# Window attention and two MLPs on one core: the sign of the weights through a parametric ReLU, and the normalising of the first items on VectorE

## The chip, the core and the metric

One core of a Trainium2 chip runs one program. The metric is the device time of one execution in microseconds (us). Three executions of the kernel before took 966.86, 967.08 and 969.48 us; their median, 967.08 us, is the time that the change is held against.

## The reference, cut to what matters

```python
# attention: q, k, v are (4 batches, 8 heads, 576 rows, 64), window 128
scores = scale * q @ k^T + bias[head]          # masked to 0 <= i - j < 128
attn = exp(scores - max(scores));  attn = attn / (sum(attn) + 1e-09)
x = (attn @ v) as 2304 tokens x 512
# first MLP, 512 -> 2048 -> 512; weights are float64
h = x @ w_in;  g = max(h, 0) + alpha * min(h, 0);  x = g @ w_out
# second MLP, 512 -> 2048 -> 512; weights are float64
h = x @ w_in2;  g = h * sigmoid(1.702 * h);  out = g @ w_out2
```

The weights of both MLPs come as float64, and the chip computes in float32. So every weight has to be turned into float32 on the chip before a matmul can use it.

## The kernel before, in words

**Items.** Attention is cut into 64 items: `u` (the first 256 query rows of a batch, or the other 320) by batch by head. Item `n` below 32 has `u` = 0. The first 16 items (`FP`) run their matmuls on plain float32 operands; from item 16 on the operands are split into a high and a low part. An item goes through these steps: `a_qk` (TensorE, scores `s`, L343 or L352 and L353), `a_bias` (VectorE, adds the bias and takes the extreme of each row, L363), `a_exp` (ScalarE, exponential with row sums, L379), `a_recip` (VectorE, L387 and L388), `a_norm` (multiplies the rows by the reciprocal), `a_trans` (TensorE, transposes into `pt`, L412), `a_pt_hi` (ScalarE copies `pt` out of PSUM, L419), `a_av` (TensorE, the product `x` with the values, L433 or L445) and, after each second head, `a_x3` (ScalarE casts the result into `xh`, L480, VectorE makes the low part `xl`, L107). Two heads fill one of four chunks of `xh`; eight items fill the 256 tokens of one batch.

**Normalising.** An item of `u` = 0 has two pieces, 128x128 and 128x256. With `"mix"`, which the first 18 items have, VectorE multiplies the small piece (L399) and ScalarE the large one (L397). With `"dve"`, all other items, VectorE does both (L399).

**Decoding weights.** A layer's weights come in 32 chunks of 128x512 float64, each loaded as pairs of 32-bit words into one of four buffers `ws` (`w_load`, L131, 512 KB). A chunk then goes through: `w_scale` (ScalarE: L147 scales the high words, read as a float, by 2^-112 into `wd`; L148 scales the low words), `w_sign` (VectorE L152: keeps the top bit of the high words alone), `w_shift` (VectorE L157: shifts `wd` left by 3, which moves the exponent into place and pushes the sign out, and ors the kept sign in), `w_add` (VectorE L162: adds the low words; after this the buffer `ws` is free for the next load), and `w_split` (ScalarE L102 or VectorE L103 makes the high part `wh`, VectorE L107 the low part `wl`).

**Stages.** A prologue of ten loop rounds runs ten items and decodes two chunks a round. Then comes the first MLP in blocks `k` of 256 tokens (the last of 512) by 16 slices `f` of the hidden width: twelve matmuls `h` (L494), the activation (ScalarE L509, VectorE L519, ScalarE L523, VectorE L107), twelve matmuls `o` (L545). One attention item goes along with every two slices. The block `k` = 0 needs items 0 to 7 (all four chunks of `xh`) and decodes the last twelve chunks of the first layer on the way; `k` = 1 needs items 8 to 15. The second layer's 32 chunks are decoded during the last block of the first MLP and during the second MLP (`h` L592, later `p` L659).

**What sets the order.** The program is recorded in the order of the code, and a scheduler with a model of the instructions' times then orders each engine's instructions once, when the program is built. On the chip each engine takes them in that order. From the last block of the first MLP on (`pin`), instructions of the decoding keep the order of the code.

Of the kernel before, what the change touches and what calls it, by code (L numbers as in the profile page):

```python
# [11 lines left out]
F32 = mybir.dt.float32  # L12
# [3 lines left out]
AF = mybir.ActivationFunctionType  # L16
ALU = mybir.AluOpType
# [48 lines left out]
def tile_window_attention__then__two_mlps(  # L66
# [13 lines left out]
    nc = tc.nc  # L80
# [32 lines left out]
    def pin(ins):  # L113
        if pinned:
            tc.keep_in_program_order(ins)
# [9 lines left out]
    wst, wtm, wt, wf = {}, {}, {}, {}  # L125
# [8 lines left out]
    def w_words(i):  # L134
        s = wst[i].bitcast(I32).rearrange("p (n t) -> p n t", t=2)
        return s[:, :, 0], s[:, :, 1]

    def w_scale(i):
        lo, hi = w_words(i)
        layer, f, part = chunks[i]  # L140
        if layer == 1 and part == 1:
            if f % 2 == 0:
                wf[f // 2] = p3["wf"].tile([P, 2, DM], I32, tag="wf", name="wf")
            wtm[i] = wf[f // 2][:, f % 2, :]
        else:
            wtm[i] = wtmp.tile([P, DM], I32, tag="wd", name="wd")
        pin(nc.scalar.mul(wtm[i].bitcast(F32), hi.bitcast(F32), 2.0**-112))  # L147
        pin(nc.scalar.mul(lo, lo.bitcast(U32), 2.0**-29))  # L148

    def w_sign(i):  # L150
        lo, hi = w_words(i)
        pin(nc.vector.tensor_scalar(hi, hi, -0x80000000, None, op0=ALU.bitwise_and))  # L152

    def w_shift(i):
        lo, hi = w_words(i)
        w = wtm[i]
        pin(nc.vector.scalar_tensor_tensor(w, w, 3, hi, op0=ALU.logical_shift_left, op1=ALU.bitwise_or))  # L157

    def w_add(i):

# [59 lines left out]

    def w(step, lim=2 * NF):

        names = ("load", "scale", "sign", "shift", "add", "split")
        i = wdone.get(step, 0)
        if i < min(lim, wdone.get(names[names.index(step) - 1], 0)):
            {"scale": w_scale, "sign": w_sign, "shift": w_shift, "add": w_add, "split": w_split}[step](i)
            wdone[step] = i + 1

    def w_ahead():
        if wdone.get("add", 0) >= 2 * NF and ("x", 0) not in p2:  # L230
            return
        i = wdone.get("load", 0)
        while i < min(wdone.get("add", 0) + NST, len(chunks)):
            w_load(i)
            i += 1
        wdone["load"] = i

    def w_decode(lim):
        w("sign", lim)
        w("shift", lim)  # L240
        w("add", lim)
        w_ahead()
        w("scale", lim)
# [79 lines left out]
    @stage  # L323
    def a_split_v(n, b, u, h, U):
        nv = (2, 4)[u]
        vr = raw_of(n)[:, UCOLS[u] - nv * D : UCOLS[u]].rearrange("p (j d) -> p j d", d=D)
        if n < FP:
            d0 = (h % 2) * D
            nc.gpsimd.tensor_copy(vzs[n % 2][:, :, d0 : d0 + D], vr)
            return  # L330
        vp = ar["v", n % 2]
        nc.scalar.copy(vp[:, :nv, :D], vr)
        sub("pool", vp[:, :nv, D:], vr, vp[:, :nv, :D])
# [49 lines left out]
    @stage  # L383
    def a_recip(n, b, u, h, U):
        s = sts[n % 2]
        m = len(U["chunks"])
        nc.vector.tensor_scalar(s[:, 8 : 8 + m], s[:, 4 : 4 + m], 1e-9, None, op0=ALU.add)  # L387
        nc.vector.reciprocal(s[:, 12 : 12 + m], s[:, 8 : 8 + m])  # L388

    @stage  # L390
    def a_norm(n, b, u, h, U, eng):
        tt, s = tts[n % 2], sts[n % 2]
        for i, (c0, rows, kk, keys) in enumerate(U["chunks"]):
            t = tt[:rows, i * 256 : i * 256 + keys]
            r = s[:rows, 12 + i : 13 + i]
            if eng == "act" or (eng == "mix" and i):
                nc.scalar.mul(t, t, r)  # L397
            else:
                nc.vector.tensor_scalar(t, t, r, None, op0=ALU.mult)  # L399
# [27 lines left out]
    @stage  # L427
    def a_av(n, b, u, h, U):
        if n < FP:
            x = st["x", n] = st["x", n - 1] if h % 2 else ps_a.tile([P, 512], F32, tag="a", name="x")  # L430
            pt, vz = pts[n % 2], vzs[n % 2]
            for j in range(2):
                nc.tensor.matmul(  # L433
                    x[:, j * P : 256], vz[:, j, :], pt[:, j * 256 : 256 + j * P],
                    start=(h % 2 == 0 and j == 0), stop=(h % 2 == 1 and j == 1), skip_group_check=True,
                )
            return
        vp = ar["v", n % 2]
        x = ps_a.tile([P, 512], F32, tag="a", name="x")
        js = (0, 1) if u == 0 else (2, 1, 3, 4)  # L440
        for i, j in enumerate(js):
            col, nq, oc = PTCOL[u][j]
            v = vp[:, j - U["k0"] // P, :]
            for k, p in enumerate((ar["pth"], ar["ptl"])):
                nc.tensor.matmul(  # L445
                    x[:, oc : oc + nq], v, p[:, col : col + nq],
                    start=(i == 0 and k == 0), stop=(i == len(js) - 1 and k == 1),
                    skip_group_check=True,
                )
        st["x", n] = x  # L450
# [283 lines left out]
    for n in range(H + 2):  # L734

        a_av(n - 2)
        a_split_v(n)
        if n + 4 < H + 2:
            a_load(n + 4)
        if n >= H:  # L740
            a_load(n + 2)
        if n + 1 < H + 2:
            a_qk(n + 1)
        a_bias(n)
        w("split")
        w("sign")
        a_exp(n)
        a_recip(n - 1)
        w("shift")
        a_norm(n - 1, "mix")  # L750
        a_trans(n - 1)
        w("add")
        w_ahead()
        w("scale")
        a_x3(n - 2)
        w("split")
        w("sign")
        w("shift")
        a_pt_hi(n - 1, 0)
        a_pt_hi(n - 1, 1)  # L760
        if n + 2 < H + 2:
            a_split(n + 2)
        w("add")
        w_ahead()
        w("scale")
    n = H + 2
# [1 line left out]
    for i in range(2):  # L768
        a_pt_lo(n - 2, i)
    a_recip(n - 1)  # L770
    a_norm(n - 1, "mix")
    a_av(n - 2)
    a_x1(n - 2)
    a_x2(n - 2)
# [5 lines left out]
    steps = [(k, f) for k in range(KM + 1) for f in range(NF)]  # L780
    for s, (k, f) in enumerate(steps):
        n = H + 2 + s // 2
        norm = "mix" if k == 0 else "dve"
        if (k, f) == (KM, 0):
            pinned.append(True)
        dec = k == 0 or k == KM
        lim = min(3 * NF, max(W1, wdone["split"]) + 3) if k else W1

        def wd(*names):
            for x in names if dec else ():  # L790
                w(x, lim)

        m = n - 1
        m1_h(k, f)
        if s % 2 == 0:
            a_trans(m)
            a_qk(n)
            a_pt_hi(m, 0)
            m1_n(k, f)
            wd("sign")  # L800
            m1_g(k, f)
            a_pt_hi(m, 1)
            a_bias(n)
            wd("shift")
            a_pt_lo(m, 0)
            a_pt_lo(m, 1)
            wd("add", "scale")
            w_ahead()
            a_split(n + 1)
            a_exp(n)  # L810
            m1_lo(k, f, "dve")
        else:
            a_av(m)
            if n == FP:
                a_parts()
            a_recip(n)
            a_split_v(n)
            a_load(n + 2)
            a_norm(n, norm)
            m1_n(k, f)  # L820
            wd("sign")
            m1_g(k, f)
            a_x1(n - 1)
            wd("shift", "scale")
            a_x2(n - 1)
            wd("add")
            w_ahead()
            m1_lo(k, f, "dve")
            a_x3(n - 1)
        if k == 0:  # L830
            w("split")
        m1_o(k - (f < LAG), (f - LAG) % NF)
        if n == NI + 1 and s % 2:
            at.close()
            p2["ps"] = ctx.enter_context(tc.tile_pool(name="ps_p", bufs=1, space=PSUM))
            p2["x", 0] = ctx.enter_context(tc.tile_pool(name="p20", bufs=1))
            pre = ExitStack()
            p2["g1"] = pre.enter_context(tc.tile_pool(name="g1", bufs=3))
            p2["n1"] = pre.enter_context(tc.tile_pool(name="n1", bufs=2))
            w_ahead()  # L840
        if k == KM:
            w("split", min(3 * NF, W1 + 2 * (f - 2)))
            if f >= 8 and f % 2 == 0:
                x2_split(0, f // 2 - 4)
            if f >= 6 and f % 2 == 0 and f < 14:
                x2_load(0, f // 2 - 3)
    for f in range(NF - LAG, NF):
        m1_o(KM, f)
    for _ in range(3):
        w("split", 3 * NF)  # L850
        wd("sign", "shift", "add", "scale")
    p1.close()
    ps_o.close()
    pre.close()
# [12 lines left out]
    for s, (j, f) in enumerate(steps):  # L867
        m2_h(j, f)
        m2_g(j, f)
        lim = 3 * NF + 8 + (2 * (f // 4) if j == last else 0)  # L870
# [93 lines left out]
```

## Time and profile before

| | before |
|---|---|
| median of 3 runs | 967.08 us |
| the profiled execution | 967.92 us |
| its span, first to last instruction | 966.1 us |
| TensorE busy | 939.6 us (97%) |
| VectorE busy | 721.6 us (75%) |
| ScalarE busy | 536.4 us (56%) |
| GpSimd busy | 89.8 us (9%) |

The engines are named PE (TensorE matmul), PEld (its weight loads), DVE (VectorE), ACT (ScalarE), POOL (GpSimd) and SP (SyncE, which issues the transfers). The profile is of one execution. A busy share of the whole span mixes stages: the slices over time, and the tables by stage made from them, tell which engine holds which stage. Matmuls overlap each other in the array, so the distance between the starts of two of them, not the duration of one, tells TensorE's pace.

### The profile page before, as it was taken

The page shows a single profiled execution, that of the slowest core. Times are in us where ns is not written, and L with a number is a line of the kernel's source. Part 1 is how long each engine was busy: PE and PEld are TensorE (multiplying, and loading weights), DVE is VectorE, ACT ScalarE, POOL GpSimd, SP SyncE. Part 2 cuts the span into 40 slices and gives each one's busy share as a digit, 9 for nine tenths or more (in the row PEclk, how much of TensorE's full clock was granted, in tenths as well). Part 3 has the DMA queues.
Part 4 walks back from the last instruction along what each step waited for, and adds up shares of the span by engine and source line. Part 5 has one row for each costly group of instructions (what it writes and reads, how often), then busy time and mean ns, then how long its engine had stood idle before and what let it go on. Part 6 is the DMA issues. An engine that isn't in the chain of part 4 may idle for free.

```text
span 966.1 us, 17886 instructions
## 1 busy us (share of the span) xinstructions
PE 939.6 (97%) x6536; PEld 871.2 (90%) x6536; DVE 721.6 (75%) x1789; ACT 536.4 (56%) x1343; POOL 89.8 (9%) x127
## 2 busy tenths in 40 slices
PE   5899999999999999999999999999999999999997
PEld 3579889999999999999988888888898889999997
DVE  6998967767888888887666864697233798878876
ACT  6987766666767667676534443564232644333433
POOL 1000021122222222222000000000000000000000
PEclk9999999999999999999999999999999999999999
DMA  8654521222222223212022335566432333443323
GB/s 266 187 185 148 184 79 56 78 72 66 89 67 88 67 66 89 67 66 89 1 69 81 124 112 182 186 219 200 155 113 88 140 140 114 142 142 113 132 85 109
DMA packets 43895, 112.44 MB, mean 116 GB/s; under 512 B 5024, under 2 KB 15008, under 8 KB 43808
## 3 DMA queue, kind: packets, MB, share of 16 engines
q1 hardware_dynamic: 43808, 111.31, 35.3%
q8 instruction: 51, 0.84, 0.3%
q14 instruction: 36, 0.29, 0.1%
HBM read 82.98 MB, written 28.31 MB: 115 GB/s over the span
## 4 chain that ended last, share of the span: by engine, by line
PE 92%; DMA 3%; ACT 2%; DVE 1%; issue 1%; SPq 0%; DVEq 0%; ACTq 0%
PE h L494 21%; PE h L592 20%; PE p L659 17%; PE o L545 17%; PE p L545 5%; PE x L445 3%; PE pt L412 3%; DMA ws<-in_w_out_dram 2%; PE s L352 1%; PE s L353 1%; PE s L343 1%; PE x L433 1%; ACT ws L148 1%; DMA ws<-in_w_in_dram 0%; ACT oh L102 0%
## 5 line engine op out<-in xcount | busy, mean ns | idle before, releaser
L494 PE MATMUL h<-xh,wh 128*128 128x256 f32 (+1 forms) x512 | 153.7, 302 | 1.0 <-ACT xh L480 0.7
L494 PE MATMUL h<-xh,wl 128*128 128x256 f32 (+1 forms) x512 | 153.6, 300 | 0.0
L494 PE MATMUL h<-xl,wh 128*128 128x256 f32 (+1 forms) x512 | 153.5, 300 | 0.1
L659 PE MATMUL p<-wh,oh 128*128 128x256 f32 x504 | 136.2, 284 | 1.0 <-ACT oh L102 0.6
L659 PE MATMUL p<-wl,oh 128*128 128x256 f32 x504 | 136.1, 283 | 0.0
L545 PE MATMUL o<-gh,wl 128*128 128x256 f32 x448 | 127.5, 286 | 0.0
L545 PE MATMUL o<-gh,wh 128*128 128x256 f32 x448 | 125.4, 286 | 0.0
L545 PE MATMUL o<-gl,wh 128*128 128x256 f32 x448 | 125.2, 281 | 0.0
L659 PE MATMUL p<-wh,ol 128*128 128x256 f32 x504 | 119.2, 284 | 1.0 <-DVE ol L107 1.0
L592 PE MATMUL h<-x2h,wh 128*128 128x512 f32 (+1 forms) x320 | 117.8, 368 | 0.0
L592 PE MATMUL h<-x2l,wh 128*128 128x512 f32 (+1 forms) x320 | 117.7, 368 | 0.0
L592 PE MATMUL h<-x2h,wl 128*128 128x512 f32 (+1 forms) x320 | 117.7, 368 | 0.0
L606 DVE TENSOR_TENSOR g<-h,sg 128x512 f32<-128x512 f32 (+1 forms) x80 | 51.0, 637 | 79.6 <-ACT sg L602 79.5
L602 ACT ACTIVATE sg<-h 128x512 f32<-128x512 f32 (+1 forms) x80 | 44.5, 556 | 107.2 <-PE h L592 106.9
L494 PEld LDWEIGHTS h<-xh,wh 128*128 128x128 f32 x512 | 97.9, 192 | 6.7 <-ACT xh L480 1.9
L494 PEld LDWEIGHTS h<-xl,wh 128*128 128x128 f32 x512 | 98.5, 192 | 5.0 <-DVE st L388 1.3
L494 PEld LDWEIGHTS h<-xh,wl 128*128 128x128 f32 x512 | 98.3, 192 | 2.9
L659 PEld LDWEIGHTS p<-wh,oh 128*128 128x128 f32 x504 | 96.4, 192 | 2.1 <-ACT oh L102 2.0
L659 PEld LDWEIGHTS p<-wl,oh 128*128 128x128 f32 x504 | 96.7, 192 | 0.1
L519 DVE SCALAR_TENSOR_TENSOR g<-n,beta,h 128x256 f32<-128x256 f32 x112 | 53.2, 476 | 46.6 <-ACT n L509 46.4
L659 PEld LDWEIGHTS p<-wh,ol 128*128 128x128 f32 x504 | 86.3, 192 | 1.7 <-DVE ol L107 1.6
L509 ACT ACTIVATE n<-h 128x256 f32<-128x256 f32 x112 | 42.8, 384 | 79.9 <-PE h L494 79.5
(107 smaller groups left out, 2270.7 us busy)
## 6 DMA issues: line engine op xcount, KB each, us to landing
ws<-in_w_in_dram SPq DMA_DIRECT2D x32, 512.0 KB, 3.6
ws<-in_w_out_dram SPq DMA_DIRECT2D x32, 512.0 KB, 3.9
raw<-in_u_dram SPq DMA_DIRECT2D x32, 512.0 KB, 3.4
g2d<-g SPq DMA_DIRECT2D x32, 512.0 KB, 3.4
gr<-g2d SPq DMA_DIRECT2D x32, 512.0 KB, 3.2
raw<-in_u_dram SPq DMA_DIRECT2D x16, 320.0 KB, 2.8
wd<-x2d SPq DMA_DIRECT2D x36, 128.0 KB, 3.0
out_dram<-ob SPq DMA_DIRECT2D x16, 256.0 KB, 3.9
```

The costliest lines, as they stand in the source:

```text
L148: pin(nc.scalar.mul(lo, lo.bitcast(U32), 2.0**-29))
L343: nc.tensor.matmul(o[:, :keys], raw[:, c0 : c0 + rows], raw[:, 256 + kk : 256 + kk + keys], start=True, stop=True)
L412: nc.tensor.transpose(banks[bank][:, dst : dst + P], src, ident)
L445: nc.tensor.matmul(x[:, oc : oc + nq], v, p[:, col : col + nq], start=(i == 0 and k == 0), stop=(i == len(js) - 1 and k == 1), skip_group_ ...
L494: nc.tensor.matmul(ph, w[:, 0, c * P : (c + 1) * P], x[:, c, r : r + n], start=(c == 0 and i == 0), stop=(c == NC - 1 and i == 2),)
L509: nc.scalar.activation(n, ph, AF.Relu, scale=-1.0)
L519: nc.vector.scalar_tensor_tensor(g, n, beta[:, f : f + 1], ph, op0=ALU.mult, op1=ALU.add)
L545: nc.tensor.matmul(o, w[:, 1, c * P : (c + 1) * P], g, start=(f == 0 and (k == KM or c % 2 == 0) and i == 0), stop=(f == NF - 1 and i == 2 ...
L592: nc.tensor.matmul(ph[:, :n], w[:, f % 2, c * P : (c + 1) * P], x[:, c, :n], start=(c == 0 and i == 0), stop=(c == NC - 1 and i == 2),)
L602: nc.scalar.activation(sg[:, :n], ph[:, :n], AF.Sigmoid, scale=1.702)
L606: nc.vector.tensor_tensor(g[:, f % 2, :n], ph[:, :n], sg[:, :n], op=ALU.mult)
L659: nc.tensor.matmul(o[:, m, :], g[:, a, m * P : (m + 1) * P], w, start=(p == 0 and m == 0 and i == 0), stop=(p == NF // 2 - 1 and i == 2), ...
```

## The change

`w_scale` uses a parametric ReLU in place of the plain multiplication of the high words: a positive value is scaled by 2^-112, a negative one by 2^-112 and by -2^32. The result is positive either way, and for a negative weight the 2^32 sets the bit that the shift by 3 brings to the place of the sign. So `w_sign` and the or in `w_shift` go; `w_shift` becomes a shift alone. And `a_norm` is `"dve"` for all items.

```diff
-        pin(nc.scalar.mul(wtm[i].bitcast(F32), hi.bitcast(F32), 2.0**-112))
+        pin(nc.scalar.activation(
+            wtm[i].bitcast(F32), hi.bitcast(F32), AF.Prelu, scale=2.0**-112, alpha=-(2.0**32)
+        ))
         pin(nc.scalar.mul(lo, lo.bitcast(U32), 2.0**-29))
-    def w_sign(i):
-        lo, hi = w_words(i)
-        pin(nc.vector.tensor_scalar(hi, hi, -0x80000000, None, op0=ALU.bitwise_and))
-
     def w_shift(i):
-        lo, hi = w_words(i)
         w = wtm[i]
-        pin(nc.vector.scalar_tensor_tensor(w, w, 3, hi, op0=ALU.logical_shift_left, op1=ALU.bitwise_or))
+        pin(nc.vector.tensor_scalar(w, w, 3, None, op0=ALU.logical_shift_left))
...
# prologue (ten items) and the items beside block k = 0
-        a_norm(n - 1, "mix")
+        a_norm(n - 1, "dve")
...
-        norm = "mix" if k == 0 else "dve"
+        norm = "dve"
...
# every call of the step "sign" goes
-        w("sign")
-            wd("sign")
```

The scheduler also orders the program anew. In the changed kernel L148 has become L150, L157 and L162 stand at L154 and L159, and the lines of the items and of the MLPs are lower by 4 (L494 is L490 there).

VectorE at the program's start, before (`tt` and `st` are an item's scores and row values, `wd` and `ws` a chunk of weights):

```order
L387 TENSOR_SCALAR st_148<-st_148 128x2
L388 RECIPROCAL st_148<-st_148 128x2
L399 TENSOR_SCALAR tt_146<-tt_146,st_148 128x128
L152 TENSOR_SCALAR ws<-ws 128x512
L157 SCALAR_TENSOR_TENSOR wd<-wd,ws 128x512
L363 ISA tt_147,st_149<-s,relht 128x128
```

and now:

```order
L383 TENSOR_SCALAR st_148<-st_148 128x2
L384 RECIPROCAL st_148<-st_148 128x2
L395 TENSOR_SCALAR tt_146<-tt_146,st_148 128x128
L395 TENSOR_SCALAR tt_146<-tt_146,st_148 128x256
L154 TENSOR_SCALAR wd<-wd 128x512
L159 ISA wd<-ws,wd 128x1024
L359 ISA tt_147,st_149<-s,relht 128x128
```

The mask of the sign is gone, the shift has one operand instead of two, and the 128x256 piece of the item stands here as a second multiplication. The addition (L162, now L159) has moved ahead of the next item's bias.

ScalarE just ahead of the fourth `xh`, with which the first batch's tokens are complete, before:

```order
L397 ACTIVATE tt_146<-tt_146,st_148 128x256
L419 COPY pt_161<-pt 128x384
L102 CAST wh_533<-wd 128x512
L148 ACTIVATE ws<-ws 128x512
L419 COPY pt_160<-pt 128x384
L147 ACTIVATE wd<-ws 128x512
L379 ACTIVATE tt_147,st_149<-tt_147,st_149 128x128
L379 ACTIVATE tt_147,st_149<-tt_147,st_149 128x256
L480 CAST xh<-x 128x256
```

and now:

```order
L150 ACTIVATE ws<-ws 128x512
L147 ACTIVATE wd<-ws 128x512
L415 COPY pt_161<-pt 128x384
L375 ACTIVATE tt_147,st_149<-tt_147,st_149 128x128
L375 ACTIVATE tt_147,st_149<-tt_147,st_149 128x256
L150 ACTIVATE ws<-ws 128x512
L102 CAST wh_474<-wd 128x512
L147 ACTIVATE wd<-ws 128x512
L476 CAST xh<-x 128x256
```

The multiplications of items (L397) are gone from this queue, and one copy `pt` and one chunk's rows that stood ahead of the fourth `xh` now stand behind it.

TensorE where item 15, the last that block `k` = 1 needs, gives its `x` (L433) and the `h` of that block begin, before:

```order
L412 MATMUL pt<-ident,tt_147 128x128
L352 MATMUL s<-kh,q 128x192
L353 MATMUL s<-kl,q 128x192
L352 MATMUL s<-kh,q 128x256
L353 MATMUL s<-kl,q 128x256
L412 MATMUL pt<-ident,tt_147 128x128 x2
L433 MATMUL x<-pt_161,vz_159 128x256
L433 MATMUL x<-pt_161,vz_159 128x128
L494 MATMUL h<-xh,wh_226 128x256
L494 MATMUL h<-xh,wh_270 128x256
```

and now, beginning with the second `o` behind the two `x` of item 15:

```order
L541 MATMUL o_736<-gl,wh_1278 128x256
L541 MATMUL o_736<-gh,wl_1279 128x256
L541 MATMUL o_736<-gh,wh_1278 128x256
L541 MATMUL o_736<-gl,wh_1278 128x256
L541 MATMUL o_736<-gh,wl_1279 128x256
L408 MATMUL pt<-ident,tt_146 128x128
L348 MATMUL s<-kh,q 128x192
L349 MATMUL s<-kl,q 128x192
L348 MATMUL s<-kh,q 128x256
L349 MATMUL s<-kl,q 128x256
L408 MATMUL pt<-ident,tt_146 128x128 x2
L490 MATMUL h<-xh,wh_225 128x256
```

Before, the first two `h` stood right behind `x`; now six `o`, four `s` and three transposes stand between them.

## Rows read from the trace of the kernel before

**Rows 1.** Profile page, busy tenths of three engines in 40 slices of 24.15 us

```profile
PE   5899999999999999999999999999999999999997
...
DVE  6998967767888888887666864697233798878876
ACT  6987766666767667676534443564232644333433
```

**Rows 2.** Windows: stretch, length; busy us of PE, PEld, DVE, ACT, POOL; clock, DMA share, GB/s

```profile
20.00:58.00 38.00, 33.06 (x97) 22.67 (x97) 34.56 (x98) 33.57 (x82) 3.03 (x7) 1.00 0.65 203
58.00:68.00 10.00, 9.85 (x37) 7.77 (x37) 9.14 (x26) 9.07 (x25) 0.79 (x2) 1.00 0.65 187
68.00:111.00 43.00, 43.00 (x345) 41.21 (x345) 38.65 (x97) 33.62 (x80) 1.11 (x3) 1.00 0.50 155
111.00:130.00 19.00, 16.57 (x108) 14.35 (x107) 13.39 (x44) 13.42 (x42) 3.38 (x7) 0.91 0.49 164
130.00:960.00 830.00, 828.01 (x5933) 779.63 (x5932) 610.79 (x1483) 434.94 (x1091) 77.90 (x92) 1.00 0.32 105
```

**Rows 3.** Chain that ended last, 0 to 60 us: start, length, what

```profile
15.32 5.73 DMA ws<-in_w_out_dram
...
51.05 4.95 DMA ws<-in_w_out_dram
```

**Rows 4.** ScalarE's groups by line and shape: count | busy us, mean ns

```profile
L379 ACT ACTIVATE tt<-tt,st 128x256 f32<-128x256 f32 x96 | 48.1, 504 | 0.4 <-DVE st L363 0.4
...
L148 ACT ACTIVATE ws<-ws 128x512 int32<-128x512 uint32 x64 | 43.2, 675 | 7.2 <-DMA ws<-in_w_out_dram 4.7 <-DMA ws<-in_w_in_dram 2.4
...
L147 ACT ACTIVATE wd<-ws 128x512 f32<-128x512 f32 x48 | 31.9, 672 | 4.9 <-DMA ws<-in_w_out_dram 2.6 <-DVE x2l L107 1.5 <-DMA ws<-in_w_in_dram 0.7
L102 ACT CAST wh<-wd 128x512 fp32r<-128x512 f32 x46 | 28.2, 616 | 3.6 <-DVE wd L162 3.6
...
L397 ACT ACTIVATE tt<-tt,st 128x256 f32<-128x256 f32 x18 | 9.1, 503 | 1.4 <-DVE st L388 1.4
...
L419 ACT COPY pt<-pt 128x384 f32<-128x384 f32 x16 | 7.6, 477 | 3.4 <-PE pt L412 3.4
```

**Rows 5.** VectorE's groups by line and shape

```profile
L162 DVE CUSTOM_DVE_ANT_0 wd<-ws,wd 128x1024 uint16<-128x1024 uint16 x48 | 32.9, 688 | 0.8
L157 DVE SCALAR_TENSOR_TENSOR wd<-wd,ws 128x512 int32<-128x512 int32 x48 | 32.8, 686 | 0.1
...
L152 DVE TENSOR_SCALAR ws<-ws 128x512 int32<-128x512 int32 x64 | 27.1, 424 | 4.4 <-ACT wd L147 4.2
...
L399 DVE TENSOR_SCALAR tt<-tt,st 128x256 f32<-128x256 f32 x78 | 24.6, 351 | 1.1
```

**Rows 6.** ScalarE's timeline, the fourth `xh`: start us, length us, engine, line, out<-in, shapes

```profile
58.39 0.39 ACT L480 CAST xh<-x 128x256 fp32r<-128x256 f32 x1
```

**Rows 7.** TensorE's timeline around 67 us

```profile
66.95 0.41 PE L494 MATMUL h<-xl,wh 128*128 128x256 f32 x1
67.16 0.41 PE L494 MATMUL h<-xh,wl 128*128 128x256 f32 x1
...
67.71 0.28 PE L494 MATMUL h<-xh,wl 128*128 128x256 f32 x1
67.83 0.28 PE L494 MATMUL h<-xh,wh 128*128 128x256 f32 x1
```

**Rows 8.** TensorE's timeline, item 15's `x` and the `h` behind it

```profile
123.88 0.92 PE L433 MATMUL x<-pt,vz 128*128 128x256 f32 x4 [0.88 <-ACT pt L419]
125.51 0.74 PE L494 MATMUL h<-xh,wh 128*128 128x256 f32 x2 [0.71 <-ACT xh L480]
...
127.33 0.41 PE L494 MATMUL h<-xh,wl 128*128 128x256 f32 x1
127.54 0.41 PE L494 MATMUL h<-xl,wh 128*128 128x256 f32 x1
...
128.74 0.51 PE L494 MATMUL h<-xh,wh 128*128 128x256 f32 x1
```

More of the change, by code (lines that the diff above doesn't have):

```diff
@@ L221, in w @@
     def w(step, lim=2 * NF):
-        names = ("load", "scale", "sign", "shift", "add", "split")
+        names = ("load", "scale", "shift", "add", "split")
         i = wdone.get(step, 0)
         if i < min(lim, wdone.get(names[names.index(step) - 1], 0)):
-            {"scale": w_scale, "sign": w_sign, "shift": w_shift, "add": w_add, "split": w_split}[step](i)
+            {"scale": w_scale, "shift": w_shift, "add": w_add, "split": w_split}[step](i)
             wdone[step] = i + 1
@@ L238, in w_decode @@
     def w_decode(lim):
-        w("sign", lim)
         w("shift", lim)
@@ L756, in tile_window_attention__then__two_mlps @@
         w("split")
-        w("sign")
         w("shift")
@@ L770, in tile_window_attention__then__two_mlps @@
     a_recip(n - 1)
-    a_norm(n - 1, "mix")
+    a_norm(n - 1, "dve")
     a_av(n - 2)
@@ L820, in tile_window_attention__then__two_mlps @@
             m1_n(k, f)
-            wd("sign")
             m1_g(k, f)
@@ L850, in tile_window_attention__then__two_mlps @@
         w("split", 3 * NF)
-        wd("sign", "shift", "add", "scale")
+        wd("shift", "add", "scale")
     p1.close()
```

## The prediction, made before the changed kernel ran

> **What bounds the kernel now.** I read the slices over time first. TensorE's first two slices stand at 5 and 8 and all others at 9, down to the last; VectorE and ScalarE are fullest in the first five slices and thin out later [rows 1]. So if time is to be had, it lies in the first 130 us. The table by stage says it sharper: from 130 to 960 us TensorE is busy for 828.01 of 830 us [rows 2]. Whatever VectorE sheds there can bring at most those 2 us, and I count nothing. From 68 to 111 us TensorE is busy all 43 us as well, with VectorE at 38.65 and ScalarE at 33.62 beside it [rows 2].
>
> Two stretches are left. From 20 to 58 us three engines are nearly full together: VectorE 34.56, ScalarE 33.57 and TensorE 33.06 of 38 us [rows 2]. This stretch ends for the first MLP with the fourth `xh` at 58.39 us [rows 6]; before it block `k` = 0 can't start in earnest. From 111 to 130 us TensorE has 16.57 of 19 us, and the granted clock reads 0.91 [rows 2]: it waits 0.88 us for item 15's `pt`, then 0.71 us for its `xh` [rows 8].
>
> TensorE's pace has to be read too. Until about 67.4 us two `h` of 256 columns start 0.21 us apart, which is 256 columns at 1.2 GHz; then 0.12 us apart, at 2.4 GHz [rows 7]. Before that rise came 9 us of mostly `h`, from the fourth `xh` on. The column of the clock shows 1.00 on both sides [rows 2], so here the spacing is what tells the level.
>
> **The change part by part.** *On VectorE.* 64 masks at 424 ns go, 27.1 us in all [rows 5]. The shift had two sources and took 686 ns. No row shows a shift with one; the mask, of the same line form with one source and the same 128x512 words, took 424, and I take that; 686 is the upper end [rows 5]. So a chunk sheds 0.424 + 0.262 = 0.69 us, both layers 64 times that, 44 us. The large piece of 18 items comes in at 351 ns, 6.3 us [rows 5].
>
> *On ScalarE.* The 18 multiplications at 503 ns go, 9.1 us [rows 4]. What Prelu costs no row shows. The nearest row is what it replaces, 672 ns. An exponential and a multiplication with the same 128x256 tile took 504 and 503 ns [rows 4], so in this trace the function made no difference, and I take 672. The lower end is 616 ns, the cast of a tile of that size [rows 4]; the upper, if each element were gone through twice, 1344 ns. The Trainium skill, "ScalarE activation tables: per-element evaluation and per-set limits", section "What a function is on this engine", says that the same operands cost the same whichever table is read; by that Prelu is 672 ns and the sum stays.
>
> *Stage to 58.39 us.* ScalarE's queue ahead of the fourth `xh`, by the two orders, loses 9 multiplications, and one each of a high scaling, a low scaling, a cast and a copy of `pt` have moved behind it: 9 x 0.503 + 0.672 + 0.675 + 0.616 + 0.477 = 7.0 us [rows 4]. VectorE's queue ahead of the fourth `xl` loses 17 masks (7.2), 17 shifts at 0.686 become 16 at 0.424 (4.9), one addition and one low part go behind it (1.4), and 10 large pieces come in (3.5), with two short instructions of at most 0.35 each: 9.3 us net [rows 5]. So both engines could bring `xh` forward by 7 us. But TensorE has the same matmuls to do ahead of item 7's `x`, but for one item's three transposes, and it was idle for only 4.9 of the 38 us [rows 2]. And loads end waits on the chain: up to 21.05 us the chain waits for a `ws` chunk, and once more for 4.95 us from 51.05 [rows 3]. The loads before 21 us don't get faster. So this term lies between 1.5 (every idle gap but a few stays) and 7.0 us; I take 4.2, near TensorE's bound, since on an engine fed by two others some idle stays.
>
> *Stage from 58 to 111 us.* Nothing: TensorE is full, and the engines beside it only get lighter, VectorE by 12 chunks x 0.69 less six large pieces x 0.351, 6 us. That it stays full is the cover under which those 6 us are worth nothing. Were it gone, the most that could be lost is what VectorE did not shed, and that is less than before.
>
> *Stage from 111 to 130 us.* By item 15's `xl`, VectorE has 32 masks (13.6) and 32 x 0.262 (8.4) behind it no more, and 17 large pieces (6.0) more: 16.0 us lighter; ScalarE is 16 x 0.503 = 8.0 us lighter. TensorE comes here only about 4 us earlier, so the item's copies should now be ready in time. The order helps as well: the first two `h` stood right behind `x`; now six `o`, four `s` and three transposes lie between. Idle there is 19 - 16.57 = 2.4 us [rows 2], and behind the second wait `h` started 0.21 us apart again, until about 128.74 us [rows 8]. With 1.2 GHz as the other level a mean clock of 0.91 is 3.4 of 19 us at half pace, which costs 1.7 us [rows 2]. I take 3.0 of these 4.1 us; 1.0 if only the wait for `xh` goes.
>
> *Sum.* 4.2 + 3.0 = 7.2 us off the profiled execution's 967.92, which is 960.7. That execution stands 0.84 us above the median of the runs, so against the median I expect 960 us.
>
> **Rivals.**
>
> A. *Start-up is held by TensorE at 1.2 GHz and by the loads.* For it: 33.06 busy of 38 us, loads on the chain to 56 us [rows 2, 3]. Against: nearly 5 us of idle are there, and both engines that feed TensorE get 7 us lighter. Then 1.5 from the first term and 1.0 from the last: 967.1 - 2.5 = 964.6.
>
> B. *The clock rises earlier.* If denser work in the prologue lifted TensorE to 2.4 GHz by 40 us, the full 7.0 us of ScalarE's bound would come, the 8.8 us from the fourth `xh` to the rise, not all of them `h`, would lose about 3.5 us [rows 6, 7], and with 3.0 at the end the time is 967.1 - 13.5 = 953.6. Against it: from 20 to 58 us TensorE was busy 87% [rows 2] and stayed at 1.2 GHz. The Trainium skill, "TensorE: Matmul & The Clock Gate", section "What's actually happening", says that the throttled state is the default and that activity releases it. The rise at 67 us agrees with that, and by it a denser prologue would give B's 953.6; that 87% busy did not release the clock before 58 us speaks for the forecast.
>
> C. *Slower: the clock rises later, or falls again.* In the changed order the first 24 `h` in a row come only after the tenth item's `x`, where before 29 `h` were already done. Each `h` or `o` at 1.2 GHz costs 0.09 us more [rows 7]. The 7.2 us are used up from 80 such matmuls on; if 110 of block `k` = 0's 384 ran so, 10 us are lost and the time is 970. For it: after 1.6 us of waits, with few `h` between, the pace halved for 3 us [rows 8]. Against it: those 24 `h` stand closer together than the ones ahead of the rise.
>
> D. *Prelu costs more than a multiplication.* At 1344 ns, 32 x 0.67 = 21 us come on to ScalarE before item 15's `xh`, 13 more than the 8.0 that leave: slower by up to 13, about 975 when half of it shows as waits. It decides from 0.43 us more each, where the 16 ahead of the fourth `xh` eat the 7.0 us.
>
> E. *The shift doesn't speed up.* At 686 ns VectorE still sheds 9.3 - 16 x 0.262 = 5.1 us by the fourth `xl`; the time is 961 to 962, inside the forecast.
>
> **How the numbers follow.** The forecast, 957 to 963.5, with E in it: 0.57. A, 963.5 to 966.5: 0.20. B: 0.09. C: 0.09. D: 0.05. A measurement of this kernel can tell about 0.3% from no change, 2.9 us, so faster means below 964.2. The forecast and B are faster, and of A somewhat less than half, 0.08, and a little of C, 0.02: 0.76. The rest of A and 0.03 of C and D: 0.15 the same. Slower: 0.09. The range leaves out most of C and D above, and the lower half of B: 955 to 966 us.
>
> **What would show it.** Right: the fourth `xh` between 52 and 56 us; item 15's `xh` not waited for; TensorE busy without a gap from there to 960 us, with the same durations by line; no row above 430 ns at the shift and about 672 at the scaling. If the fourth `xh` comes at 57 us and TensorE's idle before it is unchanged, A is right. The spacing of `h` shows B and C: 0.12 us before 50 us, or 0.21 us beyond 70. The forecast is wrong if the time gained at 130 us is not the time gained at the end: then something behind it, which I hold to be full, was not.

## The result and the profile after

The changed kernel took 953.92, 955.34, 956.68 and 957.78 us, median 956.01 us. Four runs of the kernel before beside it had a median of 966.97 us. The ratio is 0.9887, 95% interval 0.9869 to 0.9905: about 11 us less. The profiled execution took 953.92 us with a span of 952.1 us, 14.0 us less than the profiled one of before; it is the fastest of the four. So the median lies 4 us below the forecast of 960, inside the range of 955 to 966 us.

The page of the kernel after, busy time of each engine:

```profile
PE 926.4 (97%) x6536; PEld 862.7 (91%) x6536; DVE 689.1 (72%) x1743; ACT 526.9 (55%) x1325; POOL 89.5 (9%) x127
```

Compare this line with the span. Before, 966.1 us of span were 939.6 us of TensorE busy and 26.5 us idle; now 952.1 us are 926.4 busy and 25.7 idle. So of 14.0 us, 0.8 came from idle time and 13.2 from busy time, with 6536 matmuls in both. The same matmuls became faster. (The median of the runs moved by 11 us; the split is of this pair of profiles.)

The stages, of the kernel after, in the columns of [rows 2]:

```profile
20.00:58.00 38.00, 31.63 (x132) 23.07 (x132) 34.62 (x111) 35.39 (x91) 3.73 (x10) 0.96 0.78 237
58.00:68.00 10.00, 10.00 (x82) 9.46 (x81) 9.11 (x27) 9.45 (x24) 0.30 (x1) 1.00 0.64 207
68.00:111.00 43.00, 43.00 (x334) 39.96 (x333) 34.57 (x98) 32.31 (x84) 3.03 (x5) 1.00 0.50 169
111.00:130.00 19.00, 18.78 (x155) 18.30 (x155) 14.71 (x50) 13.34 (x44) 4.48 (x10) 1.00 0.32 99
130.00:940.00 810.00, 808.66 (x5772) 760.64 (x5771) 578.42 (x1407) 423.24 (x1056) 74.46 (x87) 1.00 0.33 107
```

From 20 to 58 us TensorE is busy for 31.63 us where it was 33.06 [rows 2], and yet it got through 132 recorded matmul instructions instead of 97. From 111 to 130 us the idle 2.4 us are down to 0.2 and the granted clock reads 1.00 in place of 0.91.

ScalarE's timeline of the kernel after, the fourth and the eighth `xh`, start and length first, answers to [rows 6]:

```profile
50.15 0.35 ACT L476 CAST xh<-x 128x256 fp32r<-128x256 f32 x1
...
113.36 0.37 ACT L476 CAST xh<-x 128x256 fp32r<-128x256 f32 x1
```

The eighth, before:

```profile
125.09 0.37 ACT L480 CAST xh<-x 128x256 fp32r<-128x256 f32 x1
```

The fourth came at 58.39 us before [rows 6], so it is 8.2 us earlier; the eighth is 11.7 us earlier. The rest of the 14.0 us, 2.3, lies behind the eighth.

The stretch from 20 us to the fourth `xh`, first of the kernel before, then of the kernel after:

```profile
20.00:58.39 38.39, 33.45 (x98) 22.97 (x98) 34.67 (x98) 33.96 (x83) 3.03 (x7) 1.00 0.65 202
20.00:50.15 30.15, 25.69 (x97) 18.24 (x96) 27.42 (x92) 28.18 (x73) 3.08 (x8) 0.96 0.79 241
```

TensorE was idle for 4.9 us in it before and for 4.5 now. Nearly all of the 8.2 us is that its busy time fell from 33.45 to 25.69 us; VectorE and ScalarE have less to do in it as well.

TensorE's timeline of the kernel after, from 34 to 57 us, answers to [rows 7]:

```profile
34.19 0.41 PE L490 MATMUL h<-xl,wh 128*128 128x256 f32 x1
34.40 0.41 PE L490 MATMUL h<-xh,wl 128*128 128x256 f32 x1
...
35.25 1.49 PE L429 MATMUL x<-pt,vz 128*128 128x256 f32 x4
37.01 1.10 PE L429 MATMUL x<-pt,vz 128*128 128x256 f32 x4 [0.27 <-ACT pt L415]
...
40.80 0.28 PE L490 MATMUL h<-xl,wh 128*128 128x256 f32 x1
40.91 0.28 PE L490 MATMUL h<-xh,wl 128*128 128x256 f32 x1
...
47.38 0.38 PE L490 MATMUL h<-xl,wh 128*128 128x256 f32 x1 [1.10 <-DVE xl L107]
...
47.73 0.41 PE L490 MATMUL h<-xl,wh 128*128 128x256 f32 x1
47.95 0.42 PE L490 MATMUL h<-xh,wl 128*128 128x256 f32 x1
...
51.13 0.82 PE L429 MATMUL x<-pt,vz 128*128 128x256 f32 x4
...
56.33 0.39 PE L490 MATMUL h<-xh,wh 128*128 128x256 f32 x1 [1.61 <-DVE g L515]
56.56 0.28 PE L490 MATMUL h<-xl,wh 128*128 128x256 f32 x1
56.67 0.28 PE L490 MATMUL h<-xh,wl 128*128 128x256 f32 x1
```

Read the spacing. Two `h` start 0.21 us apart at 34 us, 0.11 apart at 40.8, 0.22 apart again at 47.7, and 0.11 from 56.56 on; the four matmuls of an `x` take 1.49 us at 35 us, 1.10 at 37 and 0.82 at 51. So the clock rose to 2.4 GHz at about 37 us, was back at 1.2 from about 47.7 to 51, behind a wait of 1.1 us for `xl`, and stayed high from there. Before, it rose at 67.4 us [rows 7].

TensorE's timeline of the kernel after, item 15's `x` and its `h`, answers to [rows 8]:

```profile
112.25 0.81 PE L429 MATMUL x<-pt,vz 128*128 128x256 f32 x4
...
114.33 0.48 PE L490 MATMUL h<-xh,wh 128*128 128x256 f32 x2
114.65 0.28 PE L490 MATMUL h<-xl,wh 128*128 128x256 f32 x1
114.76 0.28 PE L490 MATMUL h<-xh,wl 128*128 128x256 f32 x1
```

Neither waits now, and the `h` stand 0.11 us apart.

How much of TensorE's work ran at 1.2 GHz follows from two windows of each kernel, busy times in the order PE, PEld, DVE, ACT, POOL. The kernel before, up to the rise and in the dip behind item 15:

```profile
0.00:67.60 67.60, 51.28 (x152) 35.42 (x153) 55.93 (x160) 54.07 (x130) 7.41 (x25) 1.00 0.72 219
125.50:128.70 3.20, 3.09 (x13) 2.68 (x13) 1.54 (x6) 1.48 (x6) 0.69 (x2) 0.52 0.57 177
```

The kernel after:

```profile
0.00:37.00 37.00, 22.83 (x65) 15.22 (x66) 25.87 (x84) 25.95 (x62) 4.77 (x19) 1.00 0.84 258
47.70:51.00 3.30, 3.03 (x13) 2.45 (x12) 3.26 (x11) 3.19 (x10) 0.30 (x1) 0.50 0.65 191
```

That is 54.4 us of busy time at the lower level before and 25.9 after: 28.5 us less. At twice the pace they take half, so 14.3 us should go; TensorE's busy time fell by 13.2. In size, the pace accounts for the gain of this pair of profiles; what brought the earlier rise is another question. The clock column doesn't show it: it reads 1.00 in the first window of either kernel, at 0.21 us spacing, and only falls in a dip behind a first rise.

### The profile page after: what moved, and what is told of

Same layout as the page of the kernel before. It is cut to its first block, busy times and chain, and to the rows that moved or that the text cites. A ratio compares the mean times of both kernels' runs of the same rounds, so it can differ in the third digit from the quotient of the medians.

```text
span 952.1 us, 17835 instructions
## 1 busy us (share of the span) xinstructions
PE 926.4 (97%) x6536; PEld 862.7 (91%) x6536; DVE 689.1 (72%) x1743; ACT 526.9 (55%) x1325; POOL 89.5 (9%) x127
## 4 chain that ended last, share of the span: by engine, by line
PE 92%; DMA 2%; ACT 2%; DVE 2%; issue 1%; SPq 0%; DVEq 0%; ACTq 0%
PE h L490 21%; PE h L588 20%; PE p L655 18%; PE o L541 17%; PE p L541 5%; PE x L441 3%; PE pt L408 3%; DMA ws<-in_w_out_dram 1%; PE s L348 1%; PE s L349 1%; PE s L339 1%; PE x L429 1%; DMA raw<-in_u_dram 0%; DVE wl L107 0%; ACT oh L102 0%
## 5 line engine op out<-in xcount | busy, mean ns | idle before, releaser
L490 PE MATMUL h<-xh,wh 128*128 128x256 f32 (+1 forms) x512 | 151.9, 298 | 1.9 <-DVE g L515 1.6
L490 PE MATMUL h<-xl,wh 128*128 128x256 f32 (+1 forms) x512 | 151.9, 297 | 1.1 <-DVE xl L107 1.1
L490 PE MATMUL h<-xh,wl 128*128 128x256 f32 (+1 forms) x512 | 152.1, 297 | 0.0
L588 PE MATMUL h<-x2h,wh 128*128 128x512 f32 (+1 forms) x320 | 117.8, 368 | 0.0
L490 PEld LDWEIGHTS h<-xl,wh 128*128 128x128 f32 x512 | 96.9, 189 | 5.9 <-issue 1.6
L490 PEld LDWEIGHTS h<-xh,wh 128*128 128x128 f32 x512 | 96.5, 189 | 5.8 <-DVE g L515 1.8
L490 PEld LDWEIGHTS h<-xh,wl 128*128 128x128 f32 x512 | 96.7, 189 | 2.9
```

The source lines that it names most:

```text
L490: nc.tensor.matmul(ph, w[:, 0, c * P : (c + 1) * P], x[:, c, r : r + n], start=(c == 0 and i == 0), stop=(c == NC - 1 and i == 2),)
L588: nc.tensor.matmul(ph[:, :n], w[:, f % 2, c * P : (c + 1) * P], x[:, c, :n], start=(c == 0 and i == 0), stop=(c == NC - 1 and i == 2),)
```

## The experiments

Two theories stood after the result. Theory 1: the lighter queues of ScalarE and VectorE together bring the fourth `xh` forward, and TensorE follows. Theory 2: the earlier rise of the clock is what the time is made of. Ratios are against runs of the kernel before beside them, with their 95% interval.

**The sign alone.** Parametric ReLU and one-source shift, the norms as before (diff against the kernel after):

```diff
-        norm = "dve"
+        norm = "mix" if k == 0 else "dve"
...
-        a_norm(n - 1, "dve")
+        a_norm(n - 1, "mix")
```

> The sign part of the change alone (Prelu, one-source shift, no mask); items 0 to 17 keep the large piece of their normalising on ScalarE. Theory 1, two engines bind the prologue together and neither part is enough: VectorE sheds its 0.69 us a chunk, ScalarE nothing; the fourth xh comes at 56 to 60 us (50.2 in the full change, 58.4 before), TensorE's matmuls stay 0.21 us apart until then, and the time is 962 to 966 us. Rival, VectorE alone bound the prologue: the fourth xh at or before 50 us and 955 us or less, since without the 17 large pieces VectorE is 6 us lighter still.

Measured 965.31 us, ratio 0.9987 (0.9974 to 1.0001). ScalarE's timeline has the fourth `xh` at 61.06 us, and the windows of this kernel are:

```profile
20.00:58.00 38.00, 30.77 (x98) 20.98 (x97) 31.15 (x92) 35.66 (x87) 3.60 (x7) 0.95 0.80 232
58.00:68.00 10.00, 8.09 (x26) 5.83 (x25) 8.37 (x21) 9.28 (x23) 1.06 (x3) 0.50 0.79 232
20.00:61.06 41.06, 32.99 (x104) 22.66 (x103) 33.93 (x98) 38.72 (x93) 4.16 (x8) 0.91 0.80 235
```

VectorE sheds 3.4 us in the first stretch against before, ScalarE gains 2.1, and `xh` is later than before, a little past the expected 60 us, while the time is as expected. The order shows why: the scheduler filled VectorE's free time with decoding, so 19 scaled chunks and 16 casts to `wh` stand ahead of the fourth `xh` on ScalarE, where before it was 17 and 13. From 20 us to that `xh` ScalarE is busy for 38.72 of 41.06 us, before for 33.96 of 38.39, after for 28.18 of 30.15; VectorE and TensorE have 7 and 8 us of idle time in it. So ScalarE sets it here. The rival that VectorE alone does it has fallen. TensorE's clock rose at about 50 us in this kernel, 17 us earlier than before and not behind the fourth `xh`, as was expected; then it fell again: from 57 to 70.7 us its matmuls show the slower pace.

Some expectations below measure an engine's queue by the sum of its instructions' durations. Neighbouring instructions overlap, so such sums are too long: before, 117.8 us on ScalarE up to the eighth `xh`, where the trace has it busy for 98.3. That a sum comes near the time of an `xh` does not show that the engine was full.

**The norms alone.** Mask and two-source shift stay (diff against the kernel before):

```diff
-        a_norm(n - 1, "mix")
+        a_norm(n - 1, "dve")
...
-        norm = "mix" if k == 0 else "dve"
+        norm = "dve"
```

> The normalising part alone: all items on VectorE; mask and two-source shift stay. Theory 1: VectorE, already full for 34.6 of 38 us, takes on 0.35 us an item, the fourth xh stays within 2 us of 58.4 us and the time is 964 to 968 us. Rival, ScalarE alone bound the prologue: with its 0.5 us an item gone the fourth xh comes by 52 us and the time is 958 us or less.

Measured 976.47 us, ratio 1.0102 (1.0086 to 1.0118), a miss: slower by 10 us where 964 to 968 was expected. The fourth `xh` came at 57.19 us, as expected, but the eighth at 133.78. Windows of this kernel:

```profile
20.00:57.19 37.19, 32.53 (x95) 22.06 (x94) 31.66 (x99) 27.73 (x70) 2.82 (x7) 1.00 0.60 179
68.00:111.00 43.00, 40.88 (x310) 37.94 (x308) 36.80 (x94) 31.00 (x76) 1.30 (x3) 1.00 0.48 148
111.00:130.00 19.00, 16.38 (x114) 14.19 (x115) 16.94 (x46) 11.71 (x30) 1.50 (x2) 1.00 0.57 178
```

Up to the fourth `xh` both engines that feed TensorE have less to do than before, ScalarE by 6 us and VectorE by 3, and yet it came only 1.2 us earlier: the clock stayed at 1.2 GHz until 69.5 us, and TensorE was busy for 32.53 of 37.19 us.

Later VectorE is at 16.94 of 19 us, and TensorE, full from 68 to 111 us before, now has gaps in both stretches. Up to the eighth `xh` VectorE was busy for 109.2 us, before 105.3, after 90.9; the eighth `xh` came 8.7 us later than before. That VectorE was just short of setting the stage from 58 to 130 us before is a reading of these numbers and not shown: its load grew by four, the rest is waits between the engines in a new order, and from 68 to 111 us it was less busy than before (36.80 us, before 38.65).

So the parts give about nothing and a loss of 10 us; together they give a gain of 11.

**ScalarE relieved in another way.** The sign alone, and ten casts to `wh` on VectorE instead of the norms (against the sign alone):

```diff
-HI_DVE = (0, 2)
+HI_DVE = (0, 2, 4, 7, 10, 13, 16, 19, 22, 25, 28, 31)
```

> The parametric ReLU and the one-source shift, with the norms still shared as before, and ten of the 32 casts to `wh` of the first layer moved from ScalarE to VectorE instead (twelve on VectorE in place of two). Theory (the pair works because the engines' queues come into balance; which work is moved off ScalarE does not matter): by the traces' durations ScalarE's queue up to the fourth `xh` is 52.3 us in place of 60.5 with the ReLU alone, and 105.4 up to the eighth; so the fourth `xh` comes at 52 to 55 us, and the time is 954 to 960 us. Rival (it is the moved norms themselves that count, since an item's exponential and its norm then no longer stand one behind the other on ScalarE): the fourth `xh` stays at 58 to 61 us and the time at 962 to 967 us.

Measured 961.18 us, ratio 0.9944 (0.9925 to 0.9962), against 0.9987 (0.9974 to 1.0001) for the sign alone: the intervals are apart, 4 us are won. The time and the fourth `xh`, 56.07 us, fall between what the two theories said. Windows and one wait of TensorE in this kernel:

```profile
20.00:58.00 38.00, 32.76 (x119) 22.94 (x117) 33.81 (x103) 35.65 (x88) 5.51 (x9) 0.78 0.81 250
58.00:68.00 10.00, 6.01 (x32) 5.67 (x33) 9.63 (x27) 10.00 (x25) 0.29 (x1) 0.66 0.65 199
```

```profile
61.99 0.58 PE L490 MATMUL h<-xh,wh 128*128 128x256 f32 x1 [4.04 <-DVE g L515]
62.37 0.41 PE L490 MATMUL h<-xl,wh 128*128 128x256 f32 x1
```

ScalarE is full for all 10 us from 58 to 68, TensorE waits 4.0 us for `g`, and behind that wait `h` start 0.21 us apart. The clock rose first at about 28 us, 9 us earlier than in the kernel after; four matmuls of an `s` show it in TensorE's timeline:

```profile
23.20 1.65 PE L339 MATMUL s<-raw 64*128 64x128 f32 x4
...
28.84 0.92 PE L339 MATMUL s<-raw 64*128 64x128 f32 x4
```

By 32.4 us `h` were 0.21 us apart again, and up to 66 us the pace changed five more times. So an early first rise alone is not the gain; the table at the end of this section has the whole time at 1.2 GHz. And balance explains part of what the norms add; why this balance is worth less than the other stays open.

**The mask's time put back.** On the kernel after, a mask with all ones ahead of each shift adds 0.42 us a chunk to VectorE and changes no value; the order is scheduled anew:

```diff
         w = wtm[i]
+        pin(nc.vector.tensor_scalar(w, w, -1, None, op0=ALU.bitwise_and))
         pin(nc.vector.tensor_scalar(w, w, 3, None, op0=ALU.logical_shift_left))
```

> The changed kernel with a mask of all ones (it changes no bit) on wd ahead of each shift: VectorE has 0.42 us a chunk to do again, ScalarE stays as light as in the change. From what was just measured, Theory 1 is that block k = 1 can begin when the longer of two queues, VectorE's and ScalarE's, has reached item 15 (summed instructions against the eighth xh: before 124.8 and 117.8 against 125.1 us, normalising alone 130.8 and 109.8 against 133.8, the change 108.8 and 109.2 against 113.4). Here VectorE's is 108.8 + 32 x 0.424 = 122.4: the eighth xh at 122 to 126 us and 963 to 968 us. Rival, the gain is TensorE's early clock: 954 to 959 us.

Measured 970.21 us, ratio 1.0039 (1.0021 to 1.0057). That is above the expected 963 to 968 us: all of the gain is gone, and a little more. The fourth `xh` came at 56.60 us and the eighth at 125.88, as expected. Windows and TensorE's waits up to 130 us (us in all, times, longest) of this kernel:

```profile
20.00:58.00 38.00, 29.56 (x95) 20.68 (x95) 33.57 (x108) 31.69 (x78) 3.51 (x7) 0.83 0.68 212
58.00:68.00 10.00, 8.97 (x36) 7.55 (x35) 9.23 (x26) 8.48 (x21) 0.30 (x1) 0.50 0.60 189
```

```profile
PE x L430 <- ACT pt L416: 9.2, 5, 4.0
```

Here the clock rose at about 38 us, much as in the kernel after, but behind a wait of 4.0 us for `pt` it was low again by 46.0 us, and `h` were 0.21 us apart until 68.7 us. An early rise is worth little if TensorE then starves: the clock alone isn't enough.

**ScalarE's time put back.** On the kernel after, a spare copy of 128x320 for each of the first 16 items:

```diff
...
+            if n < FP:
+                nc.scalar.copy(spare, pts[n % 2][:, :320])
```

> The changed kernel with a spare ScalarE copy of 128x320 (about 0.45 us, into a tile that nothing reads) behind each of the first 16 items' copy of pt: ScalarE has about 7 us to do again, VectorE stays as light as in the change. Theory 1: ScalarE's queue is 109.2 + 7 = 116 at item 15 and 3 longer at the fourth xh: fourth xh at 52 to 55 us, eighth at 117 to 120, time 959 to 964 us. Rival, VectorE alone bound the start: 954 to 958 us.

Measured 959.37 us, ratio 0.9925 (0.9906 to 0.9943), as expected; the fourth `xh` came at 55.96 us, a little past the expected 55, the eighth at 113.44, earlier than expected. The clock rose at about 49 us. TensorE's busy time is 929.4 us and its idle time 26.9: again it is more busy time, 3.0, than idle time, 1.2. That ScalarE's load doesn't matter has fallen.

**ScalarE relieved further.** On the kernel after, seven casts to `wh` on GpSimd:

```diff
+HI_POOL = (5, 9, 13, 17, 21, 25, 29)
...
-        pin(copy("dve" if i in HI_DVE else "act", h[:, part, :], w))
+        pin(copy("dve" if i in HI_DVE else "pool" if i in HI_POOL else "act", h[:, part, :], w))
```

> The changed kernel with the cast wh of seven of the first layer's 32 chunks on GpSimd, which is idle for nine tenths of the time. Theory 1: ScalarE's queue loses 7 x 0.62 = 4.3 us, about half of it ahead of the fourth xh; with VectorE's queue unchanged at 108.8 the longer of the two shrinks little at item 15, but the prologue shortens by 1 to 2 us: 953 to 956 us. Rival, GpSimd's casts are slow or in VectorE's way: 957 us or more.

Measured 956.44 us, ratio 0.9896 (0.9878 to 0.9915): no gain over the kernel after. The fourth `xh` stands at 49.97 us and the eighth at 113.40, where they were. ScalarE was not relieved by much in the stretch that counts: from 20 us to the fourth `xh` it was busy for 27.86 us, in the kernel after for 28.18.

**Spare matmuls to raise the clock.** Eight matmuls a prologue round, of 64 rows in bf16 and 256 columns, into a free bank, in the kernel before and in the kernel after:

```diff
+    def fill(n, m):
+        t = pso.tile([P, 2, T1], F32, tag="o0", name="o0")
+        r = raw_of(n)[:D, : 2 * P].bitcast(BF16).rearrange("p (c t) -> p c t", t=2)[:, :, 1]
+        for _ in range(m):
+            nc.tensor.matmul(t[:, 0, :], relht[:D, 0, :P], r, start=True, stop=True)
...
+        fill(n, 4)
...
+        fill(n, 4)
```

> The kernel before, with 8 spare bf16 matmuls of 256 columns for each of the ten rounds of the prologue, on an item's own input, into a bank whose contents are not used; they are there to keep TensorE at work. Theory 2, part of the gain is TensorE's clock that rises at 37 us instead of 67: here the matmuls should come 0.12 us apart well before 58 us, the 9 us from the fourth xh to the rise should lose 3 to 4 us, and the time is 961 to 964 us. Rival, the clock follows from the earlier work and is worth nothing by itself: within 1.5 us of before, or slower by what the 80 spare matmuls take (up to 80 x 0.21 = 17 us if none fits a gap).

> The changed kernel with the same 8 spare matmuls a round. Theory 2: TensorE keeps 2.4 GHz from about 20 us on and does not fall back near 47 us; the fourth xh comes by 48 us and the time is 951 to 954 us, with less scatter than 953.9 to 957.8. Rival, with the lighter engines TensorE is no bound any more at either clock: 955 to 958 us, or more by the spare matmuls.

The times of both came at two levels some 12 us apart. On the kernel before three of eight executions took 970 to 974 us and five 984 to 987, median 984.99; on the kernel after two of twelve took 965 and 966 us and ten 977 to 981, median 977.67. The ratios, 1.0091 (1.0051 to 1.0132) and 1.0097 (1.0068 to 1.0125), leave out the longest executions. All are slower than Theory 2 had it, and slower as the rivals allowed for. Both profiles are of executions at the upper level. The window from 20 to 58 us, first of the kernel before with the filler:

```profile
20.00:58.00 38.00, 37.72 (x130) 23.06 (x128) 23.61 (x70) 24.11 (x57) 2.40 (x5) 1.00 0.48 147
```

Then of the kernel after with it:

```profile
20.00:58.00 38.00, 37.72 (x128) 23.15 (x128) 21.76 (x72) 23.66 (x59) 1.59 (x5) 1.00 0.51 157
```

TensorE is busy for 37.72 of 38 us, and the clock rose only at about 74 and 70 us. The filler itself ran at 1.2 GHz and pushed the real work back: VectorE fell to 23.61 and 21.76 us, the fourth `xh` to 74.75 and 69.38. That makes TensorE a bound in this stretch by work that was added; it does not show that it is one without the filler, and it could not say what an early rise alone is worth.

**The kernel after once more.**

> The changed kernel once more, for its scatter (953.9 to 957.8 us so far) and for a second trace of the clock. Theory 2, the clock that rises at about 37 us is part of the gain: if this trace has TensorE at 1.2 GHz until 55 us or later, its profiled execution is 3 us or more slower than 953.9, and the fourth xh comes later than 50.2 us. Rival, the clock there is worth nothing: the same time within 1 us whatever the clock does.

Measured 957.42 us, ratio 0.9901 (0.9874 to 0.9929). Its profiled execution has a span of 954.5 us, 2.4 more than the first, with the fourth `xh` at 50.05 us, where it was. TensorE's timeline of that execution:

```profile
51.06 1.49 PE L429 MATMUL x<-pt,vz 128*128 128x256 f32 x4
...
57.12 0.50 PE L490 MATMUL h<-xh,wh 128*128 128x256 f32 x1 [1.44 <-DVE g L515]
57.41 0.42 PE L490 MATMUL h<-xl,wh 128*128 128x256 f32 x1
57.63 0.41 PE L490 MATMUL h<-xh,wl 128*128 128x256 f32 x1
...
60.62 0.30 PE L490 MATMUL h<-xl,wh 128*128 128x256 f32 x1
60.76 0.28 PE L490 MATMUL h<-xh,wl 128*128 128x256 f32 x1
```

The clock rose at about 37 us as in the first profile, so the late rise that the expectation asks about did not come. But it was low from about 47 to 54 us, where in the first profile it was back by 51, and once more behind the wait for `g`, where some 15 `h` ran 0.21 us apart. The first of them stood 0.8 us later than in the first profile; fifteen times 0.09 and 0.8 make 2.1 of the 2.4 us. The same program, so this is the clock's fall by itself: about 6 us more at 1.2 GHz go with 2.4 us of span. The rival that the clock is worth nothing has fallen, and such falls can explain part of the scatter of the changed kernel's times.

Put side by side, span = busy + idle of TensorE in each profile; the last column is the time in the first 140 us in which its timeline shows the pace of 1.2 GHz, read to about 1 us:

| kernel | span | busy | idle | at 1.2 GHz |
|---|---|---|---|---|
| before | 966.1 | 939.6 | 26.5 | 71 |
| sign alone | 963.8 | 934.5 | 29.3 | 67 |
| norms alone | 975.2 | 942.2 | 33.0 | 73 |
| sign, ten casts on VectorE | 959.1 | 929.3 | 29.8 | 52 |
| after, mask's time back | 968.6 | 937.6 | 31.0 | 65 |
| after, ScalarE's time back | 956.3 | 929.4 | 26.9 | 53 |
| after, casts on GpSimd | 953.3 | 928.0 | 25.3 | 42 |
| after | 952.1 | 926.4 | 25.7 | 41 |
| after, once more | 954.5 | 929.0 | 25.5 | 47 |

No variant in the table is faster than before by more than 1.2 us of idle time. What the faster ones gain is busy time of the same 6536 matmuls, and busy time goes with the time at 1.2 GHz. What the slower ones lose is mostly idle time.

## Why the prediction was right in its number and wrong in its mechanism

*The costs of the operations* were right. VectorE's groups of the kernel after, by line and shape, answer to [rows 5]:

```profile
L395 DVE TENSOR_SCALAR tt<-tt,st 128x256 f32<-128x256 f32 x96 | 31.0, 351 | 1.1
...
L154 DVE TENSOR_SCALAR wd<-wd 128x512 int32<-128x512 int32 x48 | 20.1, 422 | 3.5 <-ACT wd L147 3.3
```

And ScalarE's, which answer to [rows 4]:

```profile
L147 ACT ACTIVATE wd<-ws 128x512 f32<-128x512 f32 x48 | 32.5, 677 | 9.3 <-DMA ws<-in_w_out_dram 6.1 <-DVE x2l L107 2.5 <-DMA ws<-in_w_in_dram 0.7
```

The shift took 422 ns where 424 was taken, Prelu 677 where 672 was, the large piece 351 as said. Rivals D and E have fallen. By the Trainium skill, "ScalarE activation tables: per-element evaluation and per-set limits", section "What a function is on this engine", the function makes no difference; the trace agrees, with 677 ns for Prelu beside 672 for the multiplication.

*The stage to the fourth `xh`* is the step that failed. The prediction allowed 1.5 to 7.0 us and took 4.2, "near TensorE's bound, since on an engine fed by two others some idle stays". The fourth `xh` came 8.2 us earlier, at 50.15 us and not between 52 and 56. The term counted on idle time to go, and it hardly did: 4.9 us from 20 us to the fourth `xh` before, 4.5 now. The bound of some 33 busy us was a bound at 1.2 GHz only. At that pace the 33.45 us, less three transposes, would not have fitted into the 30.15 us that are left now (an estimate from these two rows), and the norms alone, with lighter feeding engines and the clock low, brought the fourth `xh` forward by only 1.2 us. With the clock up at 37 us TensorE needed 25.69 us, and the lighter queues could come through: ScalarE's busy time in the stretch fell by 5.8 us (33.96 to 28.18) and VectorE's by 7.3 (34.67 to 27.42).

This is rival B, which had a chance of 0.09 and a price of 953.6 us; the profiled execution took 953.92, the median 956.0. That the number 960 was nearly met is luck: the forecast had TensorE's pace unchanged and about half of the first term, and its range reached down far enough to take in part of B. What spoke against B was that 87% busy from 20 to 58 us had not raised the clock. But a mean over 38 us says nothing of how TensorE's work lies within it: after, the mean is lower, 83%, and the clock rose. The Trainium skill, "TensorE: Matmul & The Clock Gate", section "What's actually happening", says that activity releases the throttled state; the rise at 37 us agrees in kind, but that TensorE with the filler, busy for 37.72 of 38 us, stayed at 1.2 GHz until about 70 us is not explained by it.

*The stage from 58 to 111 us* was counted at nothing, and the profile's 43.00 of 43 us agrees. But the 9 us before the old rise at 67.4 us lay in it: two `h` that start 0.21 us apart there start 0.11 apart now. This was B's 3.5 us, and not in the sum. From the fourth to the eighth `xh` the lead grew from 8.2 to 11.7 us, 3.5 as well, though not by the clock alone: the new wait of 1.6 us for `g` at 56.33 worked against it, and the wait for `pt` ahead of item 15's `x` that is gone worked for it. The cover, that the engines beside TensorE "only get lighter", was right for the whole change; the norms alone, which put more on VectorE, lost nine microseconds in this stage and the next, so the cover was needed.

*The stage from 111 to 130 us* was right, and nearly in size: 3.0 of 4.1 us were taken, both waits are gone and the `h` behind them run 0.11 us apart; 0.2 us of idle is left, so about 3.9.

*Behind 130 us* nothing was counted, and TensorE is busy 808.66 of 810 us.

Rival A held that start-up is bound by TensorE at 1.2 GHz. The norms alone, where the clock stayed low, agree with that; the change got out of it by the clock. Rival C, a clock that falls again, is there as well, small: 47.7 to 51 us in one profile, 47 to 54 and 57.1 to 60.6 in the other, and large with the mask's time put back. In D half of 13 us would give 973.6 us and not 975; nothing hangs on it.

What stays open: what raised the clock at 37 us, and what the kernel after would take if it had not risen. The kernel after once more prices some 6 us at the lower pace with the work unchanged; no run holds the clock low throughout with the queues as light as in the kernel after, or high with the queues as before. So the lighter queues cannot be priced alone; the runs show that both engines have to be lighter, and that TensorE's pace is where the time went.

## What to carry to other kernels

Split a span into TensorE's busy and idle time before and after: if the same matmuls have become shorter, look at their spacing; here the gain was the clock, and not the idle time that the change was meant to remove. A bound worked out from busy time at 1.2 GHz isn't a floor, so price the case where it lifts at its own chance. And when two engines feed a third, take load off both: relieving one let a scheduler fill the time with work that lengthened the other's queue, and shifting load without relief made the kernel slower.

## What the runs showed of the hardware that was not expected

- The clock's first rise came at 37 us in the kernel after, 67.4 before, about 50 with the sign alone, 49 with the spare copies on ScalarE, 28 with the ten casts on VectorE, and 70 and 74 with fillers that kept TensorE busy for 37.72 of 38 us. In these runs a higher busy share did not go with an earlier rise, nor an earlier first rise with a shorter time.
- The clock fell again behind waits of 1.1 us (47.4 us), 1.4 us (57.1 us, in the second profile) and 4.0 us (mask put back), but not behind the 1.6 us at 56.33 us of the first profile. The same program did both. With the ten casts on VectorE it fell by 32.4 us behind waits of at most 0.38 us.
- The granted clock read 1.00 over stretches in which the spacing was 0.21 us for 256 columns, ahead of the first rise; in later dips it read 0.50 and 0.52.
- With the fillers the times came at two levels, 965 to 966 and 977 to 981 us on the kernel after, 970 to 974 and 984 to 987 us on the kernel before; what parts them is not known.
